# Native float32 products, DVE remainders and other beats in a transform and two-layer MLP kernel

## The chip, the cores and the metric

The kernel runs on one core of a Trainium2 chip. The metric is the device time of one execution in microseconds (us), as the median of a few runs. A core has TensorE (PE in the profile, its weight loads PEld), VectorE (DVE), ScalarE (ACT), GpSimd (POOL) and SyncE (SP), which here only issues DMAs. The engines run side by side and wait for each other through semaphores.

## What is computed

```python
def _attn_ref(x, filt_r, filt_i):              # x: 2 x 3008 x 256
    X = np.fft.rfft(x, axis=1)
    Y = X * (filt_r + 1j * filt_i)[None, :, :]
    return np.fft.irfft(Y, n=x.shape[1], axis=1).astype(np.float32)

def _moe_ref(x, w_in, w_out):                  # 6016 x 256 -> 2048 -> 256
    h = x @ w_in
    g = np.where(h >= 1, h, np.where(h <= -1, 0.0, (h + 1) ** 2 / 4))
    return (g @ w_out).astype(np.float32)

def _moe2_ref(x, w_in, w_out):                 # 6016 x 256 -> 2048 -> 256
    h = x @ w_in
    g = h * (1.0 / (1.0 + np.exp(-h)))
    return (g @ w_out).astype(np.float32)
# output = moe2(moe(attn(x, filt), moe_w_in, moe_w_out), moe2_w_in, moe2_w_out)
```

The convolution over 3008 positions is done as a transform of 47 x 64 points by matrix products; then come two layers of up and down products with an activation between them.

## The kernel before

**Precision.** A product that has to keep float32's accuracy is made in one of two ways. Native: one TensorE product of float32 operands. Split: each operand is written as a rounded part (type float32r, made by ACT) and a remainder (operand minus rounded part), and three fast products are summed: high x high, high x low, low x high. `triple` does this for the layers; `product` chooses between the two for the transform.

**Stages.** The transform works on 32 items (`items`, 16 channel chunks of 2 batches). The first batch (items 0 to 15) is transformed at the head, with native products. The second batch (items 16 to 31) is spread through the first layer as side work: per item one product `fwd_n1` (512 columns), a transpose `turn_fwd`, a product `fwd_n2` (384 columns), the filter `filter_` and `swap_add`, a product `inv_n2` (384 columns) and a transpose `turn_inv` into Z. All side products share one PSUM bank (`bank`, `side[0]`). Before the change the three side products are split ones: `split_x`, `split_st` and `split_item` make the parts in tiles named `hl`, the rounded part on ACT and the remainder on POOL; `split_mats` does it once for the matrices.

**Layers.** Token blocks 0 and 1 of layer 1 go through `up`, `act_rest`, `split_g` and `down`, one weight slice per beat (beats NB to GA), while `read_weight`, `form_weight` and `split_weight` convert layer 1's weights from 64-bit input. Then 88 steps of seven Strassen products each (`step`, `Group`): 40 of layer 1 and 48 of layer 2. A step is four beats. `rest_x2`, `sum_x` and `split_x2` prepare the tokens of the next pair. Layer 2's weights are converted in beats from L2C on (`fetch_weight` to `put_weight`), and from them `stage2`, `sums2`, `round2`, `rest2` and `store2` make the Strassen sums and their parts.

**Order.** What runs when is decided in two layers. The agenda (`at`, `due`) puts each piece of work at a beat. The `Planner` then holds some of the program back: PE's instructions stay in the order of the program, but for each of the others it picks the operation with the earliest modelled start, and one with an earlier due time if it starts little later. `Planner.cost` has the modelled durations. Every instruction is issued from line 179 (`put`), so the profile's rows are told apart by tile names. A modelled flag `port` keeps DVE operations of two SBUF operands and POOL operations apart.

Of the kernel before, what the change touches and what calls it, by code (L numbers as in the profile page):

```python
# [9 lines left out]
F32 = mybir.dt.float32  # L10
# [27 lines left out]
PMAX = 502  # L38
# [66 lines left out]
class Planner:  # L105
# [48 lines left out]
    def cost(self, engine, method, out, ins):  # L154
        n = out[3]
        psum = sum(i[4] for i in ins)
        port = False
        if method == "dma_start":
            return 0.06, 2.2 + 128 * n * 4 / 250e3, False
        if engine == "PE":  # L160
            busy = n / 2400 + 0.019 if "32r" in ins[0][5] else n / 600 + (0.067 if n < 128 else 0)
            return busy, busy + 0.19, False
        if engine == "ACT":
            busy = n / 1400 + (0.11 if psum else 0.152)
            return busy, busy + 0.15, False
        if engine == "DVE":
            busy = n / 960 + 0.065
            if method == "transpose":
                busy = 0.61
            return busy, busy + 0.14, len(ins) - psum >= (1 if method == "tensor_scalar" else 2)  # L170
        busy = n / 425 + 0.06
        return busy, busy + 0.17, True
# [133 lines left out]
def tile_fft_conv_moe_moe(  # L306
# [122 lines left out]
    def split_weight(m, f, pool):  # L429
        a = cv.pop((m, f))  # L430
        wh = pool.tile([128, 512], F32R, tag="wh", name=f"wh{m}_{f}")
        wl = pool.tile([128, 512], F32R, tag="wl", name=f"wl{m}_{f}")
        weights[m, f] = wh, wl
        nc.scalar.activation(wh, a, AF.Copy)
        (nc.vector if f in (0, 1) else nc.gpsimd).tensor_tensor(wl, a, wh.bitcast(F32), ALU.subtract)
# [30 lines left out]
    mats = {}  # L466

    def split_mats():
        for key, a in (("fwd1", fwd1), ("fwd2", fwd2), ("inv2", inv2)):
            hi, lo = (  # L470
                dp.tile([a.shape[0], 128], F32R, name=f"{key}_{s}", bufs=1) for s in ("hi", "lo")
            )
            nc.scalar.activation(hi, a, AF.Copy)
            nc.gpsimd.tensor_tensor(lo, a, hi.bitcast(F32), ALU.subtract)
            mats[key] = hi, lo

    def split_item(i, src):
        p, w = src.shape[0], src.shape[1:]
        hl = rot("raw")
        parts = [hl[:p, j, :w[0] * (w[1] if len(w) > 1 else 1)] for j in range(2)]  # L480
        if len(w) > 1:
            parts = [v.rearrange("p (d k) -> p d k", k=w[1]) for v in parts]
        nc.scalar.activation(parts[0], src, AF.Copy)
        nc.gpsimd.tensor_tensor(parts[1], src, parts[0].bitcast(F32), ALU.subtract)
        return parts

    def split_x(i):
        xt[i] = split_item(i, xt[i])

    def split_st(i):  # L490
        s = st[i]
        st[i] = split_item(i, s[:, :, :K1] if s.shape[2] > K1 else s)

    def product(out, key, matrix, src):
        if not isinstance(src, list):
            nc.tensor.matmul(out, matrix, src, start=True, stop=True)
            return
        (mh, ml), (h, l) = mats[key], src
        nc.tensor.matmul(out, mh, h, start=True, stop=False)
        nc.tensor.matmul(out, mh, l, start=False, stop=False)  # L500
        nc.tensor.matmul(out, ml, h, start=False, stop=True)

    def fwd_n1(i):
        st[i] = bank()
        product(st[i], "fwd1", fwd1, xt.pop(i))
# [10 lines left out]
    def fwd_n2(i):  # L516
        ps = bank()[:, :XS]
        src = st[i] if isinstance(st[i], list) else st[i][:, :, :K1]
        product(ps.rearrange("p (d k) -> p d k", k=K1), "fwd2", fwd2, src)
        st[i] = ps  # L520
# [27 lines left out]
    def inv_n2(i):  # L548
        zb[i] = zps[i % 2] if i < HEAD else bank().rearrange("p (d k) -> p d k", k=32)
        z = zb[i][:, :, :K1]  # L550
        if i in PRODUCT:
            y, v = st.pop(i)
            nc.tensor.matmul(z, inv2_swap, v.rearrange("p (d k) -> p d k", k=K1), start=True, stop=False)
            nc.tensor.matmul(z, inv2, y, start=False, stop=True)
            return
        product(z, "inv2", inv2, st.pop(i))
# [206 lines left out]
    def rest2(j, i):  # L763
        h, q = (flat2(j, hl, i // 2)[:, i % 2 * 448:(i % 2 + 1) * 448] for hl in (1, 0))
        nc.gpsimd.tensor_tensor(q.bitcast(F32R), q, h, ALU.subtract)
# [119 lines left out]
    late_tiles = []  # L885
# [8 lines left out]
    def first_slots():  # L894
        for tag in "gu":
            for i in range(2):
                spare(rings[tag][(turn.get(tag, 0) + 1 + i) % 2])
        spare(rings["we"][0].bitcast(F32))
        spare(wa3)

    def swap_slots():
        rings["wa"].append(wa3)
        for t in (rings["we"][0], wa3):
            retired.append(t.name)
        free[:] = [t for t in free if t.tensor.name not in retired]
        ring[:] = [r for r in ring if r is not xring2]
        nc.release(rings["xb"][1:])
        v = mp.tile([128, 2 * PMAX], F32, tag="xb1", name="sl_xb", bufs=1)
        late_tiles.append(v.name)
        spare(v, 2)  # L910

    def late_slots():
        c = late.tile([128, PMAX], F32, name="c0")
        late_tiles.append(c.name)
        spare(c)
        sets.append(late.tile([128, 2, 2, 7, 128], F32, name="w2e"))

    def raw_slots():
        retired.clear()
        spare(rings["we"][0].bitcast(F32))  # L920
        spare(rings["raw"][0].bitcast(F32), 2)

    def second_slots():
        retired.extend(late_tiles)
        free[:] = [t for t in free if t.tensor.name not in retired]
        spare(rings["wa"][0])
        rings["obl"] = [*rings["ob"][:2], *rings["wa"][1:]]
# [295 lines left out]
    for i in range(AHEAD_F, HEAD):  # L1223
# [12 lines left out]
    B1, SP = GA, 30  # L1236
    BSTAGES = (
        (-6, (load_x,)), (0, (fwd_n1, turn_fwd, split_st)), (7, (inv_n2, turn_inv)),
        (2, (fwd_n2, filter_, swap_add)), (4, (split_st,)), (1, (signs,)),
        (-1, (load_f,)), (-1, (split_x,)),  # L1240
# [6 lines left out]
    at(B1 - 5, split_mats)  # L1247
    END = B1 + SP * (n - 1 - HEAD) // 10 + 8
    L2C = GA + 62
    SOLO = (END - GA) // 4 + 1 | 1  # L1250

    for n_ in range(2, 6):
        for k in range(2):
            at(NB + 2 + 2 * (2 * (n_ - 2) + k), stage_block, n_, k)
# [5 lines left out]
    for j in range(NP):  # L1260
        t, r = ((GA - 14, 3), (GA - 6, 1))[j] if j < 2 else (GA + 4 * (j - 3), 2)
        at(t, sum_first, j)
        at(t + r, round_first, j)
        at(t + r + 1, rest_first, j)
    for f in range(NFC):
        t = L2C + 3 * f
        at(t, fetch_weight, 1, f)
        at(t + 3, read_weight, 1, f)
        at(t + 3, form_weight, 1, f)
        at(t + 5, put_weight, f)  # L1270
# [14 lines left out]
    xring2 = [rings["xb"][1][:, s] for s in range(2)]  # L1285

    def keep_slot():
        nonlocal wa3
        wa3 = rings["wa"].pop()

    wa3 = None
    at(GA - 5, keep_slot)

    def make_xring():
# [3 lines left out]
        ring[7:7] = [[x[:, s] for s in range(2)] for x in rings["xb"][:1]] + [xring2]  # L1298

    at(GA - 14, make_xring)  # L1300
    first = {"B11": -12, "B21": -11, "T2": -8, "T3": -6, "T1": -5, "B22": -3, "T4": -2}
    sums = {"T1": -10, "T2": -9, "T3": -8, "T4": -7}
    later = {"B11": 12, "B21": 14, "T2": 18, "T3": 28, "T1": 28, "B22": 29, "T4": 30}
    sums_later = {"T1": 16, "T2": 17, "T3": 20, "T4": 24}
    nine = {"B11": 12, "B21": 14, "T2": 26, "T3": 28, "T1": 29, "B22": 29, "T4": 30}
    held = END - GA - 4 * NP
    after = {"B11": held + 4, "B21": held + 5, "T2": 27, "T3": 28, "T1": 29, "B22": 29, "T4": 30}
    sums_after = {"T1": held + 6, "T2": held + 6, "T3": held + 7, "T4": held + 7}
    for p in range(len(PL)):
        t = GA + 4 * NP * (p - 1) if p else GA  # L1310
        s = t + 3 if p else GA - 13
# [7 lines left out]
        for which, d in (after if p == 2 else nine if p in (3, 4, 5) else later if p else first).items():  # L1319
            at(t + d, split_x2, p, which)  # L1320
            at(t + d + 1, rest_x2, p, which)
# [45 lines left out]
    def stages(t):  # L1367
        if t == max(NB, DONE + 1):
# [3 lines left out]
            sp = sctx.enter_context(tc.tile_pool(name="sums", bufs=1))  # L1372
            sums_.extend(sp.tile([128, 2, 384], F32R, name=f"sum{i}") for i in range(3))
# [4 lines left out]
        if t == B1 - 6:  # L1378
            nc.release(rings["raw"])
            make_raw("hl", [128, 2, 512], F32R)  # L1380
# [4 lines left out]
    def end_side():  # L1385
# [3 lines left out]
        nc.release(rings["raw"] + [t for m in mats.values() for t in m])  # L1389
        nc.release([t for tag in DP for t in rings[tag] if hasattr(t, "name")])  # L1390
        make_raw("rawb", [128, 512], I64)
# [5 lines left out]
    at(L2C - 2, swap_slots)  # L1397
    at(L2C + 3 * NFC + 8, raw_slots)
# [41 lines left out]
    for q in range(STEPS):  # L1440
# [11 lines left out]
        if q == Q2 + 1:  # L1452
# [3 lines left out]
            v = mp.tile([128, 2, PMAX], F32R, tag="xb1", name="xb2", bufs=1)  # L1456
            ring.insert(0, [v[:, s] for s in range(2)])
# [58 lines left out]
```

## Time and profile before

| | us |
|---|---|
| median of 3 runs | 1094.67 |
| lowest, highest | 1093.49, 1095.71 |
| the profiled execution | 1092.82 |
| its span in the trace | 1091.0 |
| PE busy | 1068.4 |
| DVE busy | 978.3 |
| ACT busy | 926.7 |
| POOL busy | 246.3 |

The busy time of PE is a union of matmul records that overlap: a record of 502 columns shows some 390 ns, while the next one starts about 227 ns later. A stall of PE shows as idle only where it is longer than that overlap, so the time from start to start says more than the busy share. A native float32 product stands as two records. Times in the rows are from the span's start; the layers' first beat lies near 48 us, GA near 148 us, and the side work runs from there to about 328 us.

### The profile page before, as it was taken

The page shows a single profiled execution, that of the slowest core. Times are in us where ns is not written, and L with a number is a line of the kernel's source. Part 1 is how long each engine was busy: PE and PEld are TensorE (multiplying, and loading weights), DVE is VectorE, ACT ScalarE, POOL GpSimd, SP SyncE. Part 2 cuts the span into 40 slices and gives each one's busy share as a digit, 9 for nine tenths or more (in the row PEclk, how much of TensorE's full clock was granted, in tenths as well). Part 3 has the DMA queues.
Part 4 walks back from the last instruction along what each step waited for, and adds up shares of the span by engine and source line. Part 5 has one row for each costly group of instructions (what it writes and reads, how often), then busy time and mean ns, then how long its engine had stood idle before and what let it go on. Part 6 is the DMA issues. An engine that isn't in the chain of part 4 may idle for free.

```text
span 1091.0 us, 14799 instructions
## 1 busy us (share of the span) xinstructions
PE 1068.4 (98%) x4743; PEld 869.1 (80%) x4743; DVE 978.3 (90%) x1579; ACT 926.7 (85%) x1746; POOL 246.3 (23%) x210
## 2 busy tenths in 40 slices
PE   9899989999999999999999999999999999999998
PEld 4588866777778888887888888888888888888886
DVE  7878988998777898999886779999999999999998
ACT  3588878989987989998997889889889889889885
POOL 6544636675540123324230000000000000000000
PEclk9999999999999999999999999999999999999999
DMA  9423232233311456565687452343433334332301
GB/s 352 142 78 126 96 124 92 85 98 114 127 47 46 161 176 212 177 206 182 239 283 266 145 170 83 136 140 112 148 122 116 125 107 140 130 111 102 120 20 39
DMA packets 66702, 149.76 MB, mean 137 GB/s; under 512 B 6848, under 2 KB 31552, under 8 KB 66624
## 3 DMA queue, kind: packets, MB, share of 16 engines
q1 hardware_dynamic: 66192, 148.54, 39.8%
q8 instruction: 37, 0.61, 0.2%
q14 instruction: 41, 0.34, 0.1%
q10 hardware_dynamic: 432, 0.27, 0.1%
HBM read 113.42 MB, written 35.37 MB: 136 GB/s over the span
## 4 chain that ended last, share of the span: by engine, by line
PE 77%; DVE 10%; ACT 9%; issue 2%; DMA 1%; POOL 0%; SPq 0%; DVEq 0%; ACTq 0%; POOLq 0%
PE h L179 39%; PE o_a L179 21%; PE o_b L179 17%; DVE gl L179 2%; ACT gh L179 2%; ACT u L179 1%; DVE wa L179 1%; ACT g L179 1%; DMA Z<-in_x_dram 1%; DVE u L179 1%; ACT wa L179 1%; DVE h L179 1%; DVE g L179 1%; ACT sl_xb L179 1%; ACT we L179 1%
## 5 line engine op out<-in xcount | busy, mean ns | idle before, releaser
L179 PE MATMUL h<-xr,ur 128*128 128x502 f32 (+1 forms) x792 | 220.8, 389 | 0.0
L179 PEld LDWEIGHTS h<-xr,ur 128*128 128x128 f32 x792 | 149.0, 189 | 31.2 <-ACT sl_g L179 0.4
L179 PE MATMUL o_a<-gl,wh 128*128 128x502 f32 (+1 forms) x358 | 139.6, 390 | 1.3 <-DVE gl L179 1.3
L179 PE MATMUL o_a<-gh,wh 128*128 128x502 f32 (+1 forms) x358 | 139.9, 391 | 0.0
L179 PE MATMUL o_a<-gh,wl 128*128 128x502 f32 (+1 forms) x358 | 139.6, 390 | 0.0
L179 PE MATMUL o_b<-gl,wh 128*128 128x502 f32 (+1 forms) x316 | 123.5, 391 | 1.1 <-DVE gl L179 1.0
L179 PE MATMUL o_b<-gh,wh 128*128 128x502 f32 (+1 forms) x316 | 123.6, 391 | 0.0
L179 PE MATMUL o_b<-gh,wl 128*128 128x502 f32 (+1 forms) x316 | 123.2, 390 | 0.0
L179 DVE TENSOR_TENSOR gl<-sl_g,gh 128x502 fp32r<-128x502 f32 (+1 forms) x137 | 90.9, 673 | 5.9 <-ACT gh L179 5.7
L179 ACT ACTIVATE gh<-sl_g 128x502 fp32r<-128x502 f32 (+1 forms) x137 | 83.9, 618 | 10.8 <-PE o_a L179 5.8
L179 PE MATMUL h<-xr,wh 128*128 128x502 f32 (+1 forms) x288 | 89.7, 393 | 1.0 <-ACT h L179 0.5
L179 PE MATMUL h<-xr,sum 128*128 128x502 f32 (+1 forms) x312 | 88.3, 391 | 0.9 <-ACT wa L179 0.5
L179 PEld LDWEIGHTS o_a<-gl,wh 128*128 128x128 f32 x358 | 67.4, 188 | 14.9 <-DVE gl L179 1.9
L179 PEld LDWEIGHTS o_a<-gh,wl 128*128 128x128 f32 x358 | 67.3, 188 | 13.7
L179 PEld LDWEIGHTS o_a<-gh,wh 128*128 128x128 f32 x358 | 67.5, 188 | 13.1
L179 PEld LDWEIGHTS o_b<-gl,wh 128*128 128x128 f32 x316 | 59.5, 188 | 14.0 <-DVE gl L179 2.7
L179 PEld LDWEIGHTS h<-xr,sum 128*128 128x128 f32 x312 | 58.5, 188 | 14.5 <-ACT wa L179 1.8
L179 PEld LDWEIGHTS o_b<-gh,wl 128*128 128x128 f32 x316 | 59.5, 188 | 12.2
L179 PEld LDWEIGHTS o_b<-gh,wh 128*128 128x128 f32 x316 | 59.5, 188 | 11.5
L179 PEld LDWEIGHTS h<-xr,wh 128*128 128x128 f32 x288 | 53.2, 188 | 14.8 <-ACT h L179 1.2
L179 ACT ACTIVATE u<-h 128x502 f32<-128x502 f32 (+1 forms) x94 | 54.8, 582 | 10.6 <-PE h L179 8.2
L179 ACT ACTIVATE u<-u 128x502 f32<-128x502 f32 (+1 forms) x100 | 61.9, 619 | 1.8 <-DVE u L179 0.6
(411 smaller groups left out, 2701.7 us busy)
## 6 DMA issues: line engine op xcount, KB each, us to landing
ur<-w2u SPq DMA_DIRECT2D x48, 896.0 KB, 4.6
f<-in_filt_dram SPq DMA_DIRECT2D x32, 384.0 KB, 3.8
sum<-w1s SPq DMA_DIRECT2D x32, 384.0 KB, 3.1
w2u<-w2s SPq DMA_DIRECT2D x10, 448.0 KB, 4.1
Z<-in_x_dram SPq DMA_DIRECT2D x16, 256.0 KB, 5.6
raw<-in_moe_w_in_dram SPq DMA_DIRECT2D x16, 256.0 KB, 2.7
raw<-in_moe_w_out_dram SPq DMA_DIRECT2D x16, 256.0 KB, 2.9
xin<-in_x_dram SPq DMA_DIRECT2D x16, 256.0 KB, 3.1
```

The lines of the kernel that those rows point to most:

```text
L179: op = Op(engine, lambda: call(*args, **kwargs), busy, until, port)
```

## The change

- The side products become native: `split_x`, `split_st`, `split_item`, `split_mats` and `product` go, with the `hl` tiles. `inv_n2` of an item comes 4 beats after its `fwd_n1` instead of 7 (`INV`), and the side work ends 3 beats earlier (`END`).
- Two kinds of remainder go from POOL to DVE: `split_weight` for slices 2 to 15 of layer 1, and `rest2` for layer 2.
- Layer 2's weights are converted from GA + 50 instead of GA + 62 (`L2C`), one slice every 3.5 beats instead of 3.
- The planner's durations are set anew: POOL, the DVE transpose and DVE's tensor_scalar.
- The stage blocks 2 to 5 are made one per beat instead of one every two; the first pair's sums and parts (`first`, `sums`) and the first weight sums are spread over some 22 beats before GA instead of 12; `make_xring` moves from GA - 14 to GA - 23. The list `nine` goes.
- SBUF slots: one `raw` tile and a new tile `c0` are slots from the start; `keep_slot`, `swap_slots` and `raw_slots` go, and both `xb` tiles stay in the ring of token parts.

```diff
@@ cost
             if method == "transpose":
-                busy = 0.61
+                busy = 0.62
+            elif method == "tensor_scalar":
+                busy = n / 1920 + 0.07
             return busy, busy + 0.14, len(ins) - psum >= (1 if method == "tensor_scalar" else 2)
-        busy = n / 425 + 0.06
+        busy = n / 430 + 0.1
@@ split_weight
-        (nc.vector if f in (0, 1) else nc.gpsimd).tensor_tensor(wl, a, wh.bitcast(F32), ALU.subtract)
+        nc.vector.tensor_tensor(wl, a, wh.bitcast(F32), ALU.subtract)
@@ the transform's products
-        nc.scalar.activation(parts[0], src, AF.Copy)
-        nc.gpsimd.tensor_tensor(parts[1], src, parts[0].bitcast(F32), ALU.subtract)
...
-        nc.tensor.matmul(out, mh, h, start=True, stop=False)
-        nc.tensor.matmul(out, mh, l, start=False, stop=False)
-        nc.tensor.matmul(out, ml, h, start=False, stop=True)
...
-        product(st[i], "fwd1", fwd1, xt.pop(i))
+        nc.tensor.matmul(st[i], fwd1, xt.pop(i), start=True, stop=True)
...
-        product(ps.rearrange("p (d k) -> p d k", k=K1), "fwd2", fwd2, src)
+        nc.tensor.matmul(ps.rearrange("p (d k) -> p d k", k=K1), fwd2, st[i][:, :, :K1], start=True, stop=True)
...
-        product(z, "inv2", inv2, st.pop(i))
+        nc.tensor.matmul(z, inv2, st.pop(i), start=True, stop=True)
@@ rest2
-        nc.gpsimd.tensor_tensor(q.bitcast(F32R), q, h, ALU.subtract)
+        nc.vector.tensor_tensor(q.bitcast(F32R), q, h, ALU.subtract)
@@ the agenda
-    B1, SP = GA, 30
+    B1, SP, INV = GA, 30, 4
     BSTAGES = (
-        (-6, (load_x,)), (0, (fwd_n1, turn_fwd, split_st)), (7, (inv_n2, turn_inv)),
-        (2, (fwd_n2, filter_, swap_add)), (4, (split_st,)), (1, (signs,)),
-        (-1, (load_f,)), (-1, (split_x,)),
+        (-6, (load_x,)), (0, (fwd_n1, turn_fwd)), (INV, (inv_n2, turn_inv)),
+        (2, (fwd_n2, filter_, swap_add)), (1, (signs,)), (-1, (load_f,)),
     )
-    END = B1 + SP * (n - 1 - HEAD) // 10 + 8
-    L2C = GA + 62
-    SOLO = (END - GA) // 4 + 1 | 1
+    END = B1 + SP * (n - 1 - HEAD) // 10 + INV + 1
+    L2C = GA + 50
+    SOLO = (END - GA) // 4 + 2 | 1
-            at(NB + 2 + 2 * (2 * (n_ - 2) + k), stage_block, n_, k)
+            at(NB + 1 + 2 * (n_ - 2) + k, stage_block, n_, k)
-        t, r = ((GA - 14, 3), (GA - 6, 1))[j] if j < 2 else (GA + 4 * (j - 3), 2)
+        t, r = ((GA - 18, 3), (GA - 8, 3))[j] if j < 2 else (GA + 4 * (j - 3), 2)
-        t = L2C + 3 * f
+        t = L2C + 7 * f // 2
-    at(GA - 14, make_xring)
-    first = {"B11": -12, "B21": -11, "T2": -8, "T3": -6, "T1": -5, "B22": -3, "T4": -2}
-    sums = {"T1": -10, "T2": -9, "T3": -8, "T4": -7}
+    at(GA - 23, make_xring)
+    first = {"B11": -22, "B21": -20, "T2": -16, "T3": -13, "T1": -10, "B22": -7, "T4": -4}
+    sums = {"T1": -20, "T2": -19, "T3": -18, "T4": -17}
```

## Rows read from the trace of the kernel before

**Rows 1.** The page: busy time in us, share of the span and instructions by engine.
```profile
PE 1068.4 (98%) x4743; PEld 869.1 (80%) x4743; DVE 978.3 (90%) x1579; ACT 926.7 (85%) x1746; POOL 246.3 (23%) x210
```

**Rows 2.** Windows: length; PE, PEld, DVE, ACT, POOL busy (count); clock; DMA; GB/s.
```profile
48.60:61.00 12.40, 9.87 (x43) 8.01 (x42) 9.84 (x16) 8.92 (x16) 3.88 (x3) 0.86 0.39 129
61.00:136.00 75.00, 75.00 (x372) 63.80 (x371) 65.44 (x101) 62.89 (x120) 40.55 (x31) 1.00 0.30 102
136.00:148.00 12.00, 9.79 (x42) 7.23 (x41) 11.57 (x22) 10.76 (x23) 6.35 (x6) 1.00 0.47 166
148.00:316.00 168.00, 158.15 (x687) 125.61 (x687) 145.61 (x229) 145.84 (x275) 97.90 (x85) 1.00 0.30 97
316.00:580.00 264.00, 263.07 (x1224) 219.51 (x1223) 232.97 (x372) 241.59 (x463) 67.69 (x51) 1.00 0.55 186
600.00:1040.00 440.00, 440.00 (x1938) 364.56 (x1937) 413.10 (x686) 383.64 (x718) 0.00 (x0) 1.00 0.36 125
```

**Rows 3.** PE's largest wait in 148:316: for whom, total us, times, longest.
```profile
PE h L179 <- DVE y L179: 3.2, 3, 1.5
```

**Rows 4.** Timeline of PE, split side products: start, length, instruction, count.
```profile
152.08 0.40 PE L179 MATMUL h<-hl,fwd_lo 128*128 128x512 f32 x1
152.31 0.39 PE L179 MATMUL o_a<-gh,wh 128*128 128x502 f32 x1
...
161.17 0.51 PE L179 MATMUL h<-hl,fwd_hi 128*128 128x384 f32 x2
161.52 0.33 PE L179 MATMUL h<-hl,fwd_lo 128*128 128x384 f32 x1
```

**Rows 5.** Timeline of PE at the head, native products of the first batch.
```profile
29.45 1.02 PE L179 MATMUL h<-Z,fwd 128*128 128x512 f32 x2
30.30 0.81 PE L179 MATMUL h<-t,dft_sb 128*128 128x384 f32 x2
30.95 0.81 PE L179 MATMUL o_b<-y,dft_sb 128*128 128x384 f32 x2
31.59 1.02 PE L179 MATMUL h<-Z,fwd 128*128 128x512 f32 x2
```

**Rows 6.** Window, instructions on tile hl alone: length, PE, PEld, ACT, POOL busy.
```profile
148.00:316.00 168.00, 35.83 (x138) 24.73 (x138) 24.24 (x44) 54.11 (x44) 1.00 0.30 97
```

**Rows 7.** Timeline of POOL, then of DVE, in 442:445.
```profile
442.55 1.16 POOL L179 TENSOR_TENSOR w2e<-w2e 128x448 fp32r<-128x448 f32 x1
...
442.78 1.47 DVE L179 TENSOR_TENSOR gl<-g,gh 128x502 fp32r<-128x502 f32 x1
...
444.75 0.67 DVE L179 TENSOR_TENSOR gl<-h,gh 128x502 fp32r<-128x502 f32 x1
```

**Rows 8.** Groups of POOL that move: busy, mean ns, idle before and its releaser.
```profile
L179 POOL TENSOR_TENSOR w2s<-w2s 128x448 fp32r<-128x448 f32 x20 | 26.1, 1331 | 41.8 <-DMA w2s<-w2d 14.8 <-ACT h L179 7.9 <-ACT g L179 6.8
L179 POOL TENSOR_TENSOR wl<-wa,wh 128x512 fp32r<-128x512 f32 x14 | 19.1, 1366 | 26.8 <-ACT wh L179 26.8
```

**Rows 9.** Timeline of DVE before the layers' first products, and PE's wait there.
```profile
43.17 0.75 DVE L179 TENSOR_SCALAR wa<-wa 128x512 f32<-128x512 f32 x2
44.92 0.72 DVE L179 STREAM_TRANSPOSE Z<-o_b 128x512 f32<-128x512 f32 x1 [1.00 <-PE o_b L179]
45.56 0.65 DVE L179 SCALAR_TENSOR_TENSOR wa<-wa,we 128x512 int32<-128x512 int32 x1
...
50.85 1.70 DVE L179 TENSOR_TENSOR wl<-wa,wh 128x512 fp32r<-128x512 f32 x2
...
PE h L179 <- DVE wl L179: 2.5, 1, 2.5
```

**Rows 10.** Timelines of DVE, ACT and POOL: one item between its two last products.
```profile
181.63 1.01 DVE L179 TENSOR_TENSOR y<-h,f 128x384 f32<-128x384 f32 x2
...
189.33 0.53 ACT L179 ACTIVATE s<-y 64x384 f32<-64x384 f32 x1
...
190.07 1.45 POOL L179 TENSOR_TENSOR s<-y,s 128x384 f32<-128x384 f32 x1
```

More of the change, by code (lines that the diff above doesn't have):

```diff
@@ L464, in load_f @@
         nc.sync.dma_start(ft[i], filt[c])
[L466 to L482, printed above, removed]
-        nc.scalar.activation(parts[0], src, AF.Copy)
-        nc.gpsimd.tensor_tensor(parts[1], src, parts[0].bitcast(F32), ALU.subtract)
[L485 to L498, printed above, removed]
-        nc.tensor.matmul(out, mh, h, start=True, stop=False)
-        nc.tensor.matmul(out, mh, l, start=False, stop=False)
-        nc.tensor.matmul(out, ml, h, start=False, stop=True)
     def fwd_n1(i):
         st[i] = bank()
-        product(st[i], "fwd1", fwd1, xt.pop(i))
+        nc.tensor.matmul(st[i], fwd1, xt.pop(i), start=True, stop=True)
     def turn_fwd(i):
@@ L517, in fwd_n2 @@
         ps = bank()[:, :XS]
-        src = st[i] if isinstance(st[i], list) else st[i][:, :, :K1]
-        product(ps.rearrange("p (d k) -> p d k", k=K1), "fwd2", fwd2, src)
+        nc.tensor.matmul(ps.rearrange("p (d k) -> p d k", k=K1), fwd2, st[i][:, :, :K1], start=True, stop=True)
         st[i] = ps
@@ L884, in tile_fft_conv_moe_moe @@
     Q2 = NP * L2P
-    late_tiles = []
+    c0 = []
     free, retired, groups, parts, banks, touched = [], [], {}, {}, {}, {}
@@ L897, in first_slots, with late_slots, free_slot @@
                 spare(rings[tag][(turn.get(tag, 0) + 1 + i) % 2])
-        spare(rings["we"][0].bitcast(F32))
[L899 to L921, printed above, removed]
+        spare(rings["raw"].pop(0).bitcast(F32), 2)
+        spare(c0[0])
+    def late_slots():
+        sets.append(late.tile([128, 2, 2, 7, 128], F32, name="w2e"))
+    def free_slot():
+        spare(rings["we"][0].bitcast(F32))
     def second_slots():
-        retired.extend(late_tiles)
+        retired.append(c0[0].name)
         free[:] = [t for t in free if t.tensor.name not in retired]
@@ L1246, in tile_fft_conv_moe_moe @@
                 at(t + d, fn, i)
-    at(B1 - 5, split_mats)
-    END = B1 + SP * (n - 1 - HEAD) // 10 + 8
-    L2C = GA + 62
-    SOLO = (END - GA) // 4 + 1 | 1
+    END = B1 + SP * (n - 1 - HEAD) // 10 + INV + 1
+    L2C = GA + 50
+    SOLO = (END - GA) // 4 + 2 | 1
     for n_ in range(2, 6):
         for k in range(2):
-            at(NB + 2 + 2 * (2 * (n_ - 2) + k), stage_block, n_, k)
+            at(NB + 1 + 2 * (n_ - 2) + k, stage_block, n_, k)
     pools = {}
@@ L1283, in tile_fft_conv_moe_moe @@
         at(Y - 24 + 4 * (t // 2), load_down, t)
[L1285 to L1292, printed above, removed]
     def make_xring():
@@ L1297, in make_xring @@
         ring.extend([xr[:, i, s] for s in range(2)] for i in range(8))
-        ring[7:7] = [[x[:, s] for s in range(2)] for x in rings["xb"][:1]] + [xring2]
-    at(GA - 14, make_xring)
-    first = {"B11": -12, "B21": -11, "T2": -8, "T3": -6, "T1": -5, "B22": -3, "T4": -2}
-    sums = {"T1": -10, "T2": -9, "T3": -8, "T4": -7}
+        ring[7:7] = [[x[:, s] for s in range(2)] for x in rings["xb"]]
+    at(GA - 23, make_xring)
+    first = {"B11": -22, "B21": -20, "T2": -16, "T3": -13, "T1": -10, "B22": -7, "T4": -4}
+    sums = {"T1": -20, "T2": -19, "T3": -18, "T4": -17}
     later = {"B11": 12, "B21": 14, "T2": 18, "T3": 28, "T1": 28, "B22": 29, "T4": 30}
     sums_later = {"T1": 16, "T2": 17, "T3": 20, "T4": 24}
-    nine = {"B11": 12, "B21": 14, "T2": 26, "T3": 28, "T1": 29, "B22": 29, "T4": 30}
     held = END - GA - 4 * NP
-    after = {"B11": held + 4, "B21": held + 5, "T2": 27, "T3": 28, "T1": 29, "B22": 29, "T4": 30}
+    after = {"B11": held + 4, "B21": held + 5, "T2": 27, "T3": 28, "T1": 28, "B22": 29, "T4": 30}
     sums_after = {"T1": held + 6, "T2": held + 6, "T3": held + 7, "T4": held + 7}
@@ L1310, in tile_fft_conv_moe_moe @@
         t = GA + 4 * NP * (p - 1) if p else GA
-        s = t + 3 if p else GA - 13
+        s = t + 3 if p else GA - 24
         at(s, load_pair, p)
@@ L1318, in tile_fft_conv_moe_moe @@
             at(t + d, sum_x, p, which)
-        for which, d in (after if p == 2 else nine if p in (3, 4, 5) else later if p else first).items():
+        for which, d in (after if p == 2 else later if p else first).items():
             at(t + d, split_x2, p, which)
@@ L1372, in stages @@
             sp = sctx.enter_context(tc.tile_pool(name="sums", bufs=1))
+            c0.append(sp.tile([128, PMAX], F32, name="c0"))
             sums_.extend(sp.tile([128, 2, 384], F32R, name=f"sum{i}") for i in range(3))
@@ L1377, in stages @@
             fixed["ws"] = rawp.tile([128, 384], F32, tag="ws", name="ws", bufs=1)
-        if t == B1 - 6:
-            nc.release(rings["raw"])
-            make_raw("hl", [128, 2, 512], F32R)
     def begin_side():
@@ L1388, in end_side @@
         rings["obs"] = rings["ob"]
-        nc.release(rings["raw"] + [t for m in mats.values() for t in m])
         nc.release([t for tag in DP for t in rings[tag] if hasattr(t, "name")])
-        make_raw("rawb", [128, 512], I64)
         dctx.close()
@@ L1396, in tile_fft_conv_moe_moe @@
     at(END, end_side)
-    at(L2C - 2, swap_slots)
-    at(L2C + 3 * NFC + 8, raw_slots)
+    at(L2C + 3 * NFC + 8, free_slot)
     for q in range(NP, NP * L2P):
@@ L1455, in tile_fft_conv_moe_moe @@
             sctx.close()
-            v = mp.tile([128, 2, PMAX], F32R, tag="xb1", name="xb2", bufs=1)
-            ring.insert(0, [v[:, s] for s in range(2)])
             gp = ctx.enter_context(tc.tile_pool(name="gp", bufs=1))
```

## The prediction, made before the changed kernel was run

> **What bounds the kernel.** I read the page first. PE is busy for 98% of the span and DVE for 90% [rows 1], so PE sets the time and DVE is close behind. An average hides the stages, so I read the windows next. In 600:1040 PE starts 1938 matmuls in 440 us, 0.227 us each, with no idle time [rows 2]: layer 2 runs at PE's pace and the change hardly touches it. I use that pace as a ruler. The loss of a stage is its length minus what its matmuls would take at full pace.
>
> In 148:316, the side transform, 687 matmuls stand in 168 us [rows 2]. 138 of them are side products [rows 6]. Their pace is on the timeline: a pass of 512 columns takes 0.23 us to the next start, and two passes of 384 take 0.35 us [rows 4]. The 138 are 48 of 512 columns and 90 of 384: 48 x 0.23 + 90 x 0.175 = 26.8 us. The other 549 take 549 x 0.227 = 124.6 us. Together that is 151.4, so **16.6 us are lost** in this stage; only 9.9 of them show as idle. The largest item among PE's waits there is DVE's `y`, the filter of the side work, 3.2 us [rows 3]. ACT and DVE are both busy for 146 of the 168 us [rows 2]: the losses are queues in front of two full engines.
>
> Three smaller places: 136:148 has 42 matmuls in 12 us, 9.5 at full pace, a loss of 2.5 us. In 48.6:61 PE waited 2.5 us for DVE's `wl` [rows 9], and the granted clock averages 0.86 over 12.4 us [rows 2]. Against the levels 2.4 and 1.2 GHz that is 28% of the window, 3.5 us, at the lower one, which costs half of that, 1.7 us. In 316:580 only 0.9 us are idle [rows 2].
>
> **The change part by part.** *Native products.* At the head the same shapes run native: 30.30 - 29.45 = 0.85 us for 512 columns, then 0.65 and 0.64 for 384 [rows 5], 2.14 per item. Split, an item costs 3 x 0.23 + 6 x 0.175 = 1.74. So PE gets 0.40 us more on each of 16 items: **+6.5 us**, all on the path, since PE is the bound. This term is sure.
>
> *The parts of the side work go.* In 148:316 the `hl` tiles hold ACT for 24.2 us and POOL for 54.1 us [rows 6]. Without them ACT is busy for 122 of 168 us (72%, it was 87%) and POOL for 44 instead of 98. DVE's own work stays, yet it gains too: a `gl` remainder on DVE took 1.47 us while POOL ran 442.55 to 443.71, and 0.67 just after [rows 7]. DVE waited for POOL's instruction to end. With over half of POOL's time gone, over half of such waits go. Each item also loses three steps of two engines between its products. What does that give back of the 16.6 us? At most nearly all (16). At the least those losses that have nothing to do with the parts; I put that end at 4. DVE still stands near 85%, and the side products still share one bank whose release waits for DVE, so some losses stay. I take two thirds, **-11 us**, nearer to the upper end, because ACT drops well below full and DVE's waits for POOL shrink at the same time.
>
> *The inverse product comes 3 beats earlier.* It waits for filter, swap and sum. In the trace this chain ran from 181.63 to 191.52 us, 9.9 us, while its own steps are 1.01 + 2 x 0.53 + 1.45 = 3.5 us [rows 10]; the rest is queueing that cost nothing with five beats between the two products. An item of three beats takes some 168 / 16 = 10.5 us, so the two beats that remain are 7 us. The planner picks by due time, so the chain should move up. I cost it at nothing; the cover is 3.5 us of slack, and if it goes, PE stands behind `inv_n2`, since its order is fixed. That is a rival below.
>
> *Remainders from POOL to DVE.* 14 of layer 1 and 32 of layer 2 (20 stand in the row, 12 more on another tile) took POOL 1.37 and 1.33 us each [rows 8]. On DVE one costs at most the 0.67 us of a `gl` [rows 7]: 14 x 0.67 = 9.4 us and 32 x 0.67 x 448/502 = 19 us. In return DVE no longer waits for them. Most of the first lie in 61:136, where DVE is busy for 65.4 of 75 us including such waits [rows 2]; most of the second in 316:580, with 233 of 264. Both still fit. I cost it at 0, with bounds of -1 and +4 for layer 2's part.
>
> *Before GA.* Stage blocks come earlier, the first pair's parts are spread over more beats. The loss of 2.5 us in 136:148 comes with DVE busy for 11.6 of 12 us [rows 2]. Spreading should ease it, but the 9.4 us of remainders arrive just ahead. I cost it at 0, between -2.5 and +3.
>
> *The first weight.* PE's 2.5 us at 48.6 wait for `wl` of slice 0, whose chain passes the row at 45.56, which stands on DVE behind a transpose that had to wait 1.00 us for PE [rows 9]. The planner models a tensor_scalar of 512 elements at 512/960 + 0.065 = 0.60 us; two of them took 0.75 [rows 9]. With the new 0.34 it sees DVE free some 0.8 us earlier and may put that row ahead of the transpose. If it does, wait and slow clock go, -4.2 us at most; if the order stays, 0. I take half, **-2.1**.
>
> *The rest at nothing.* The conversion's DMAs (two loads and a store per slice, on SP's queue) start 12 beats earlier. They move ahead of stores and loads of the same queue where no transfer shows among PE's longer waits, and layer 2's start is 30 us away. One slot more early and two fewer late matter only if a group waits for a slot, and none shows. If a slot or a load does bind, it falls into the +4 above.
>
> **The sum**: 6.5 - 11 - 2.1 = -6.6 us. The profiled execution took 1092.82 us and would come to 1086.2. It lies 1.85 us below the median of the runs, so I add that back: 1094.67 - 6.6 = **1088.1 us**. All low ends: 6.5 - 16 - 1 - 2.5 - 4.2 = -17.2, 1077. All high ends: 6.5 - 4 + 4 + 3 + 0 = +9.5, 1104.
>
> **Rivals.** *The inverse product becomes the wait.* If the chain keeps 7.9 us or so, PE stands 0.9 us for each of 16 items, +14 on the forecast: 1102. For it speaks the 9.9 us now; against it, that due times shorten it and that ACT and POOL have room. It decides from a chain of 7 us on.
>
> *PE pays and nothing comes back.* The side work stalls for DVE and the shared bank as before, and the change does not do what lighter ACT and POOL promise: 1094.7 + 6.5 = 1101. For it speaks that the longest wait is one for DVE [rows 3], whose own work stays; against it, DVE's waits for POOL.
>
> *Half comes back.* 8 us instead of 13 meet the 6.5: 1093.
>
> *DVE becomes the bound.* In 61:136 there are 9.6 us of room [rows 2]; 9.4 us of remainders and several 0.67 us parts of the first pair come in. From the point where DVE's work exceeds the stage, the surplus goes to PE: some 5 us at the most, 1093, and with as much again in 316:580, 1098. Against it speak the waits for POOL that vanish. The Trainium skill, Perfetto Trace Analysis, section Optimizing Scalar/DVE Operations, says that with a saturated DVE work may be offloaded, even to GpSimd; by that the change moves work the wrong way. The same section adds that the two share a read port, so that moving between them might not help. The trace agrees with that addition (1.47 against 0.67 us [rows 7]), so this rival gets a small chance.
>
> **How the numbers follow.** Forecast, 1079 to 1092: 0.61. Below that, when the losses go almost wholly: 0.05. Half comes back: 0.10. DVE bound: 0.08, split between no change and slower. Inverse product: 0.09. Nothing back: 0.07. Some 0.2%, 2.2 us, is about what a measurement of this kernel can tell from no change. Faster by more: 0.61 + 0.05 = 0.66. Within: 0.10 + 0.04 = 0.14. Slower: 0.04 + 0.09 + 0.07 = 0.20. The range leaves out 0.05 below and most of the last two cases above: 1079 to 1100.
>
> **What would show it.** In the changed profile the side products stand at 0.86 and 0.65 us to the next start. The side stage should lose under 8 us beside them, with ACT below 80%. PE's wait for `y` should shrink; waits of `h` for `s` or `ob`, POOL's sums, would show the first rival. Waits for `wl` in 61:136 would show DVE as the bound. At 48 us the wait for `wl` is gone or stays. 600:1040 should keep 0.227 us per matmul; if that moved, the prediction would be wrong in a place that I did not look at.

## The result and the profile after

| | before | after |
|---|---|---|
| median of 4 runs, us | 1094.13 | 1076.91 |
| lowest, highest | 1093.49, 1095.71 | 1076.50, 1077.55 |
| span of the profiled execution | 1091.0 | 1075.8 |

The ratio is 0.9841, with a 95% interval of 0.9824 to 0.9858: 17.2 us less, where 6.6 had been forecast. The sign was right; the time lies below the range of 1079 to 1100. The two profiled executions, which the rows come from, differ by 15.3 us (1092.82 and 1077.55). Some 1 to 2 us of the 17.2 (an estimate) are TensorE at its lower clock in other executions of the kernel before: 31 of 55 that were run beside the experiments had a mean granted clock of 0.998 or more and a median of 1093.1 us, 19 had 0.996 or less and 1094.9, and the changed kernel's eight all had 0.999 or 1.00.

The page of the changed kernel, its line of busy times, against [rows 1]. POOL's time has halved; PE has 48 instructions less (144 records of split side products became 96 of native ones) and the same busy time.

```profile
PE 1067.3 (99%) x4695; PEld 862.9 (80%) x4695; DVE 962.1 (89%) x1625; ACT 901.3 (84%) x1695; POOL 122.7 (11%) x113
```

Windows of the changed kernel, for [rows 2] (columns as there; the stages begin up to 6 us earlier). In the side stage, the fourth row, PE is busy for 166.5 of 168 us instead of 158.2; ACT, POOL and DVE all have less to do. Ahead of it, the first row has full clock and no idle time, and in the second PE shows no idle time either, with DVE busy for 65.6 of 68 us.

```profile
49.20:61.60 12.40, 12.40 (x74) 11.03 (x73) 10.28 (x19) 11.61 (x21) 3.46 (x3) 1.00 0.27 91
61.60:129.60 68.00, 68.00 (x330) 57.49 (x329) 65.56 (x119) 60.54 (x116) 20.63 (x17) 1.00 0.33 107
129.60:141.60 12.00, 11.60 (x52) 9.28 (x50) 11.95 (x25) 8.63 (x18) 2.91 (x4) 1.00 0.51 185
141.60:309.60 168.00, 166.54 (x671) 125.71 (x672) 136.94 (x228) 130.38 (x243) 41.95 (x40) 1.00 0.32 104
600.00:1040.00 440.00, 439.99 (x1938) 364.46 (x1938) 417.53 (x694) 385.50 (x722) 0.00 (x0) 1.00 0.35 121
```

PE's waits in that side stage, for [rows 3]: the wait for `y` went from 3.2 us to 0.4.

```profile
PE h L181 <- DVE gl L181: 1.2, 2, 0.7
PE h L181 <- DVE y L181: 0.4, 1, 0.4
```

A native product in the changed kernel's timeline of PE, for [rows 5]. It is read differently from the head: the next matmul starts in the records 0.46 us after the product and then lasts 0.80 instead of 0.39, so part of the product hides in it. To the second next start it is 167.75 - 166.66 = 1.09 us; less one pace of 0.227 that is 0.86 for 512 columns, as priced.

```profile
166.66 1.02 PE L181 MATMUL h<-xin,fwd 128*128 128x512 f32 x2
167.12 0.80 PE L181 MATMUL o_b<-gh,wh 128*128 128x500 f32 x1
167.75 0.39 PE L181 MATMUL o_b<-gl,wh 128*128 128x500 f32 x1
```

DVE before the layers' first products, timeline, for [rows 9]. The row that formed the first weight (SCALAR_TENSOR_TENSOR, at 45.56 before) now stands ahead of the transpose, at 44.43, and `wl` follows at 47.98 instead of 50.85. PE no longer waits for it.

```profile
44.43 0.68 DVE L181 SCALAR_TENSOR_TENSOR wa<-wa,we 128x512 int32<-128x512 int32 x1
45.52 0.72 DVE L181 STREAM_TRANSPOSE Z<-o_b 128x512 f32<-128x512 f32 x1 [0.41 <-PE o_b L181]
...
47.98 0.69 DVE L181 TENSOR_TENSOR wl<-wa,wh 128x512 fp32r<-128x512 f32 x1
```

**Where the time went, stage by stage.** For this table I took every matmul's time to the next start, subtracted its shape's pace (0.226 us for 502 columns, 0.43 and 0.323 for one of the two records of a native product of 512 and 384, the others likewise), and summed what is left by stage. GA is the start of the first Strassen step. "All but native" and the columns behind it are experiments that follow below. The side stage runs from GA to its last side product.

| lost us in | before | after | all but native | native alone | durations alone | remainders alone | beats alone |
|---|---|---|---|---|---|---|---|
| head | 4.4 | 5.0 | 4.3 | 5.1 | 5.1 | 4.4 | 4.6 |
| first 13 us of the layers | 4.6 | 0.5 | 0.5 | 5.7 | 0.4 | 4.6 | 1.9 |
| from there to GA - 12 us | 1.2 | 0.9 | 0.9 | 1.2 | 1.7 | 1.4 | 9.5 |
| last 12 us before GA | 3.0 | 0.7 | 0.0 | 1.8 | 1.0 | 2.3 | 1.3 |
| side stage | 18.3 | 4.2 | 19.6 | 5.8 | 23.2 | 22.6 | 19.9 |
| side stage to layer 2 | 5.3 | 3.6 | 4.0 | 5.4 | 7.4 | 3.3 | 5.4 |
| layer 2 | 3.8 | 3.8 | 3.8 | 3.8 | 3.7 | 3.8 | 3.8 |

Before to after: 40.6 - 18.7 = 21.9 us less lost, 6.5 more for native products: 15.4, and the spans differ by 15.2.

A loss counted in this way holds the time that TensorE spends at its lower clock level, 1.2 GHz. In the side stage the granted clock was 1.00 before and after. "All but native", the durations alone and the remainders alone had 0.98, 0.99 and 0.97 there: 6.8, 3.4 and 10.2 us at the lower level, of which half is lost, 3.4, 1.7 and 5.1 us. With the remainders alone the clock fell behind waits of PE for DVE's `gl` of 2.1 us (it stood at 0.54 in 148.5:156) and 2.7 us.

### The profile page after: what moved, and what is told of

It is laid out like the page before. It is cut to its first block, busy times and chain, and to the rows that moved or that the text cites. A ratio compares the mean times of both kernels' runs of the same rounds, so it can differ in the third digit from the quotient of the medians.

```text
span 1075.8 us, 14491 instructions
## 1 busy us (share of the span) xinstructions
PE 1067.3 (99%) x4695; PEld 862.9 (80%) x4695; DVE 962.1 (89%) x1625; ACT 901.3 (84%) x1695; POOL 122.7 (11%) x113
## 4 chain that ended last, share of the span: by engine, by line
PE 93%; DVE 3%; ACT 2%; DMA 1%; issue 0%; POOL 0%; SPq 0%; DVEq 0%; ACTq 0%; POOLq 0%
PE h L181 48%; PE o_a L181 24%; PE o_b L181 21%; ACT u L181 1%; DVE gl L181 1%; DMA f<-in_filt_dram 1%; DVE wa L181 1%; DVE h L181 1%; ACT gh L181 0%; DVE xr L181 0%; DMA fwd<-in_dft_dram 0%; DVE ws L181 0%; ACT raw L181 0%; DVE Z L181 0%; DVE y L181 0%
## 5 line engine op out<-in xcount | busy, mean ns | idle before, releaser
L181 PE MATMUL h<-xr,ur 128*128 128x502 f32 (+1 forms) x816 | 227.9, 389 | 0.0
L181 PEld LDWEIGHTS h<-xr,ur 128*128 128x128 f32 x816 | 153.4, 188 | 32.3 <-ACT sl_g L181 0.4
L181 PE MATMUL o_a<-gh,wh 128*128 128x502 f32 (+1 forms) x358 | 147.8, 413 | 0.0
L181 PE MATMUL o_b<-gh,wh 128*128 128x502 f32 (+1 forms) x316 | 130.8, 414 | 0.0
L181 PE MATMUL h<-xr,sum 128*128 128x502 f32 (+1 forms) x336 | 94.5, 390 | 0.1
L181 PEld LDWEIGHTS o_a<-gh,wh 128*128 128x128 f32 x358 | 67.5, 189 | 16.6 <-issue 1.4
L181 PEld LDWEIGHTS o_a<-gh,wl 128*128 128x128 f32 x358 | 67.4, 188 | 14.1
L181 PE MATMUL h<-xr,wh 128*128 128x502 f32 (+1 forms) x240 | 74.4, 391 | 0.1
L181 PEld LDWEIGHTS h<-xr,sum 128*128 128x128 f32 x336 | 63.3, 189 | 13.5 <-ACT u L181 0.5
L181 POOL TENSOR_TENSOR wa<-wa,raw 128x512 int32<-128x512 int32 x32 | 46.1, 1440 | 185.6 <-DVE wa L181 142.0
L181 DVE TENSOR_TENSOR gl<-h,gh 128x502 fp32r<-128x502 f32 (+1 forms) x84 | 56.7, 674 | 9.1 <-ACT gh L181 8.3
```

The source lines that it names most:

```text
L181: op = Op(engine, lambda: call(*args, **kwargs), busy, until, port)
```

## The experiments

Each median is compared with runs of the kernel before on the same chip (1092.9 to 1094.3 us). Four theories went in. S: making the side parts is the cause. P: the planner's old durations are. L: POOL's instructions keep DVE waiting. B: a backlog from before GA is.

### One edit alone on the kernel before

Native products alone: the split steps leave the agenda, `product` finds no parts.

```diff
-        (-6, (load_x,)), (0, (fwd_n1, turn_fwd, split_st)), (7, (inv_n2, turn_inv)),
-        (2, (fwd_n2, filter_, swap_add)), (4, (split_st,)), (1, (signs,)),
-        (-1, (load_f,)), (-1, (split_x,)),
+        (-6, (load_x,)), (0, (fwd_n1, turn_fwd)), (7, (inv_n2, turn_inv)),
+        (2, (fwd_n2, filter_, swap_add)), (1, (signs,)), (-1, (load_f,)),
...
-    at(B1 - 5, split_mats)
```

> The kernel before with native side products alone: the parts (hl tiles) are not made, the inverse product stays 7 beats after the first, nothing else changes. Theory S (the parts were the cause: ACT's and POOL's time on them and the longer chain): PE loses at most 3 us in the side stage instead of 16.6 and pays 6.5 more, so about 1087 us. Theory P (the planner's old durations misplace the side work, with or without parts): the losses stay and PE pays, about 1100 us. Theory L (it is POOL's hold on DVE that costs, and native takes half of POOL's time in the stage away): half of the loss goes, about 1092 us.

Measured 1085.9 us, a ratio of 0.9931 (0.9913 to 0.995) on 1093.4. The trace is that of a second run of the same kernel, which took 1087.4:

> The kernel before with native side products alone, again, for its trace. The time should be near 1086. If the theory of POOL's hold is right, the side stage loses 5 to 7 us instead of 18, the wait for wl at 48 us and its 4 us stand as before, and the loss between the side stage and layer 2 stands at 5.

The side stage loses 5.8 us instead of 18.3, and the other stages nearly what they lost before. The time is just below what S expected (1087). P, which expected 1100, falls, and L's "half of the loss" (1092) was too little. This edit alone brings 7.5 of the 17.2 us: -12.5 in the side stage, +6.5 on PE, and the rest lies within the scatter of the executions (the second run was 1.5 us longer).

The durations alone (the first hunk of the diff), the remainders alone (`split_weight`, `rest2`), the beats alone (stage blocks, `first`, `sums`, the first weight sums, `make_xring`, the first `load_pair`):

> The kernel before with the new modelled durations alone. Theory S: only the order at 48 us changes, the first wl is in time and wait and slow clock go there: -4 us, about 1090. Theory P: the side stage loses less too, -10 us or more, 1084 or below. Theory L: as S.

> The kernel before with the remainders of layer 1's slices and of layer 2's Strassen sums on DVE alone. Theory S: no change in the side stage, within 1.5 us of before. Theory L: DVE gains more from the locks that go than the remainders cost it, -2 to -4 us, in 61:136 and 316:580. If DVE were the bound there: +3 to +6 us.

> The kernel before with the new beats before GA alone (stage blocks one per beat, first sums and parts spread over 22 beats, the ring of parts earlier). Theory S: only the 2.5 us of 136:148 can go, about 1092. A theory B, that the backlog built up before GA runs on into the side stage: -6 us or more, 1088 or below. If DVE and ACT are too full in 85:136 for the earlier parts: +2 us.

Measured 1093.4 (ratio 1.0000, 0.999 to 1.0009), 1095.4 (1.0009, 0.9995 to 1.0024) and 1098.5 (1.005, 1.0035 to 1.0065). The durations do remove the 4.2 us at the first weight and 2.0 in the last 12 us before GA, but the side stage takes 4.9 back (1.7 of it is the clock) and the stretch behind it 2.1. The remainders alone do gain 2.0 us in that stretch, where most of them lie, but lose 4.3 in the side stage, where 5.1 us go to the lower clock. The beats alone lose 8.3 us more in the beats up to GA - 12, and 4.1 more up to GA in all; of the 9.5 us lost there 5.9 are one wait, for a converted weight, and some 3.6 the lower clock behind it (0.95 granted over 78 us). PE's waits of that kernel in 61.8:139.9:

```profile
PE h L179 <- ACT wh L179: 5.9, 1, 5.9
```

So none of these three gains anything alone, where S had expected 4 us of the durations and L 2 to 4 of the remainders. B falls: with the durations alone the layers lose 3.1 us before GA instead of 8.8, and the side stage loses more and not less.

### All but one

> The kernel before with the new durations, both kinds of remainder on DVE and the new beats before GA, but with the split side products. Theory F (the side stage is full as long as the parts are made, and gives back there what is gained ahead of it): head and beats before GA lose some 6 us less than before, the side stage more, and the time stays at 1091 to 1095. A theory A (the edits add up, native only its own share of 8): 1076.9 + 8 = 1085.

Measured 1087.2 (0.9941, 0.9925 to 0.9958), between the two theories. 7.4 us less are lost in the layers before GA, and the side stage loses 19.6, 1.3 more than before (3.4 of it is the clock). So most was kept: "a full side stage gives it all back" was too strong. That the remainders alone lose 4.3 us more there is covered by the clock; of the 4.9 with the durations alone it covers 1.7, and the rest is not explained. PE's longest waits in it are still those for DVE's `gl` and `y`.

The changed kernel with one part undone:

> The changed kernel with the old modelled durations. Theory F: now nothing is given back, so the wait and the slow clock at 48 us return in full, +4, and the order before GA costs +1: about 1082. Theory A: +0 to +1, as the durations alone brought 0.0 to the kernel before: 1077 to 1078.

> The changed kernel with both kinds of remainder back on POOL. Theory L2 (the earlier beats need DVE free of POOL's locks, since the new beats alone lost 8 us more in the beats up to GA - 12 than before): +6 to +10, 1083 to 1087, lost in 62:130. If the remainders on DVE are neutral, as they were alone: 1076 to 1078.

> The changed kernel with the old beats before GA. If spreading the first pair's work is what empties the stretch before GA: the loss of 2 to 3 us in the last 12 us before GA returns, 1079 to 1080. If the native side work and the remainders do that by themselves: within 1 us of 1077.

Measured 1079.4, 1080.3 and 1077.2 us, against 1076.9 (1076.7 on a third chip, below). Old durations cost 2.5, between the two theories; their interval (0.985 to 0.9879) just overlaps that of the changed kernel. DVE takes the rows of the first weight in the old order again, behind the transpose, and the wait for the first `wl` returns, but as 1.2 us instead of 2.5, and with no fall of the clock. The remainders on POOL cost 3.4 (0.9875, 0.986 to 0.9889), about half of the least that L2 expected, 1.6 of it up to GA - 12. The beats cost or bring nothing once the rest is there, though alone they had cost 5.

### What in the side parts costs

The base is the kernel before with new durations, remainders on DVE, new beats before GA and native products (`c_native`), everything but the inverse product's place, layer 2's beats, the slots and the list `nine`.

> The kernel before with the new durations, remainders on DVE, the new beats before GA and native side products, the parts not made; the inverse product stays 7 beats after the first, layer 2's weights and the slots stay as before. If native is what empties the side stage, with or without the earlier inverse product: 1076 to 1079, the side stage loses 4 to 6 us. If the inverse product's place and layer 2's beats have a share: 1080 or more.

Measured 1078.1, as the first theory expected. What it lacks is worth 1.2 us at most as measured; the ratio's interval (0.9836 to 0.9866) overlaps that of the changed kernel, so it is not shown to be worth anything. Then the side parts are made again, but nobody reads them (the products stay native):

```diff
-        xt[i] = split_item(i, xt[i])
+        split_item(i, xt[i])
...
-        st[i] = split_item(i, s[:, :, :K1] if s.shape[2] > K1 else s)
+        split_item(i, s[:, :, :K1] if s.shape[2] > K1 else s)
```

> As c_native, but the side parts are still made, on ACT and POOL, and nobody reads them. Theory W (the time that the parts take on ACT and POOL, with POOL's hold on DVE, is the cause): the side stage loses 12 us or more again, 1085 or above. Theory K (the longer chain from one side product to the next is the cause): as c_native, within 2 us.

Measured 1091.9, +13.9 us, for work that nothing waits for. The longer chain is not the cause, since the products no longer pass through the parts; making them is. Then each engine by itself:

```diff
 c_act_only
-        nc.gpsimd.tensor_tensor(parts[1], src, parts[0].bitcast(F32), ALU.subtract)
 c_pool_only
-        nc.scalar.activation(parts[0], src, AF.Copy)
-        nc.gpsimd.tensor_tensor(parts[1], src, parts[0].bitcast(F32), ALU.subtract)
+        nc.gpsimd.tensor_tensor(parts[1], src, src, ALU.subtract)
```

> As c_native, with ACT's rounded parts made and unused, POOL's remainders not made. If ACT's fullness is the cause: close to c_parts_unused. If POOL's hold on DVE is: close to c_native, +1 to +2 us.

> As c_native, with a subtraction on POOL for each side part (source minus itself, unused), ACT's rounded parts not made. If POOL's hold on DVE is the cause: +6 us or more over c_native. If ACT's fullness is: +1 to +2 us.

Measured 1079.4 (+1.3) and 1088.0 (+9.9). One window, 148:300, of `c_native`, then `c_act_only`, then `c_pool_only`, columns as in [rows 2]. ACT takes 137.5 of 152 us in the second, 90%, and PE hardly notices. In the third ACT has least to do, and PE loses 5 us of busy time. DVE's instructions get longer there: 129.29 us for 197 of them, 0.656 on average, against 124.76 for 208, 0.600. Of the 9.9 us 1.7 are the lower clock (3.4 us of it, behind the wait of 2.2 us for `y` below). The two prices do not add up to 13.9. One reason may be that a source minus itself is shorter than the real remainder: 1.02 us each on POOL in this window, against 1.26 in `c_parts_unused`.

```profile
148.00:300.00 152.00, 150.21 (x608) 113.86 (x607) 124.76 (x208) 120.28 (x220) 41.75 (x39) 1.00 0.34 105
```

```profile
148.00:300.00 152.00, 149.96 (x604) 112.98 (x604) 122.69 (x207) 137.53 (x264) 41.01 (x39) 1.00 0.33 105
```

```profile
148.00:300.00 152.00, 145.13 (x571) 107.02 (x570) 129.29 (x197) 114.14 (x208) 84.90 (x80) 0.99 0.33 103
```

PE's longest waits in the same window, of `c_native`, then of `c_pool_only`: the longest are for DVE.

```profile
PE h L181 <- DVE t L181: 1.3, 1, 1.3
PE h L181 <- DVE y L181: 0.4, 1, 0.4
```

```profile
PE h L181 <- DVE y L181: 2.9, 3, 2.2
PE h L181 <- DVE t L181: 1.8, 2, 1.4
```

Does POOL keep DVE waiting, or is its own queue too long for the side chain? The same places on POOL and the same tiles, modelled with the same duration and the same `port` flag, but written only:

```diff
-        nc.gpsimd.tensor_tensor(parts[1], src, src, ALU.subtract)
+        n = parts[0].shape[1] * (w[1] if len(w) > 1 else 1)
+        nc.gpsimd.memset(hl[:p, :, :n].bitcast(F32), 0.0)
```

> As c_pool_only, but each of the 48 POOL subtractions is a memset of both halves of the same unused tile, modelled with the same duration: POOL's queue is as long in the plan, nothing is read. If POOL's reads hold DVE: back near c_native, within 3 us of 1078. If POOL's longer queue delays the side chain: near c_pool_only, 1085 or above.

Measured 1079.9, +1.8 instead of +9.9. Its window, columns as above:

```profile
148.00:300.00 152.00, 149.19 (x598) 111.40 (x597) 123.34 (x206) 118.54 (x217) 69.27 (x77) 1.00 0.33 104
```

The memsets are shorter (0.81 us on average; the subtractions took 0.83 to 1.04 undisturbed and 1.02 on average), so POOL's queue is shorter too, and the time alone does not rule it out. But DVE's instructions are back at 0.599 us on average, as they were without any work of POOL on the side parts. How much of the 8 us the shorter queue gave is open. Two timelines show single ones. `c_pool_only`, POOL then DVE, twice: beside a subtraction a `gl` of two SBUF operands takes 1.46 us; another, whose `h` lies in PSUM, takes 0.64.

```profile
198.18 1.03 POOL L181 TENSOR_TENSOR hl<-xin 128x512 fp32r<-128x512 f32 x1
198.29 1.46 DVE L181 TENSOR_TENSOR gl<-wa,gh 128x500 fp32r<-128x500 f32 x1
...
265.74 0.83 POOL L181 TENSOR_TENSOR hl<-s 128x384 fp32r<-128x384 f32 x1
265.81 0.64 DVE L181 TENSOR_TENSOR gl<-h,gh 128x502 fp32r<-128x502 f32 x1
```

`c_pool_memset`, POOL then DVE: beside a memset a `gl` of two SBUF operands takes 0.67, as if alone. The whole traces agree: the 17 `gl` of two SBUF operands that start while POOL runs a subtraction or another reading instruction in `c_pool_only` took 0.70 us at least and 1.19 in the median, the 10 with an operand in PSUM at most 0.68, and the 7 beside a memset in `c_pool_memset` at most 0.67.

```profile
259.61 1.42 POOL L183 MEMSET hl<- 128x768 f32 x2
...
260.35 0.67 DVE L183 TENSOR_TENSOR gl<-u,gh 128x500 fp32r<-128x500 f32 x1
```

The Trainium skill, SBUF — State Buffer, section Who interferes with whom, says just this: a DVE instruction with two SBUF inputs contends with a GpSimd instruction that reads SBUF, and not with one that only writes. These rows agree in both halves.

### Does DVE have room for the parts?

The split products kept, their remainders on DVE, the other edits as in `b_all_but_native`:

```diff
-        nc.gpsimd.tensor_tensor(parts[1], src, parts[0].bitcast(F32), ALU.subtract)
+        nc.vector.tensor_tensor(parts[1], src, parts[0].bitcast(F32), ALU.subtract)
```

> The kernel before with new durations, new beats before GA and all remainders on DVE, those of the side parts too; the side products stay split, so PE keeps its 6.5 us. If POOL's hold was all and DVE has room for some 25 us more in the side stage: 1071 to 1074. If DVE becomes full, at 83% before it: the side stage loses 8 us or more, 1076 to 1086.

Measured 1091.7, worse than with the remainders on POOL (1087.2) and above both theories. The side stage loses 25.3 us. Its window 148:300:

```profile
148.00:300.00 152.00, 141.23 (x594) 108.69 (x593) 136.61 (x231) 126.22 (x238) 39.57 (x36) 0.99 0.29 97
```

So the parts can't be had for nothing on either engine, and PE's 6.5 us for native products are the cheapest of the three ways tried. That DVE is full at 137 of 152 us, 90%, is not shown: in 600:1040 of the changed kernel it is busy for 95%, and PE does not idle. PE's longest waits here are all for DVE (`wa` and `gl` 2.0 us each, `hl` 1.8, `y` 1.7); whether DVE lacks the time or takes its work in the wrong order was not tested.

### Is anything left?

The changed kernel with the sign products of the side items on DVE, then the swap's sums too, and the changed kernel again:

```diff
-        nc.gpsimd.tensor_tensor(v, v, sgn.unsqueeze(1).to_broadcast([128, DC, K1]), ALU.mult)
+        engine = nc.gpsimd if i < HEAD else nc.vector
+        engine.tensor_tensor(v, v, sgn.unsqueeze(1).to_broadcast([128, DC, K1]), ALU.mult)
...
-            nc.gpsimd.tensor_tensor(s, yf, s, ALU.add)
+            nc.vector.tensor_tensor(s, yf, s, ALU.add)
```

> The changed kernel with the sign products of the side items on DVE instead of POOL (16 of some 1.1 us on POOL, 0.5 us on DVE). If POOL's hold on DVE is still what costs in the side stage: -1 to -3 us, 1074 to 1076. If the rest is DVE's own work: 0 to +1.

> The changed kernel with the sign products and the swap sums of the side items on DVE (32 instructions of some 1.1 us on POOL, 0.5 us on DVE). If POOL's hold is all that is left: the side stage loses 2 to 3 us instead of 4.2, 1074 to 1076. If DVE is full with them (15 us more in a stage where it was busy for 126 of 152): as the changed kernel or above, 1077 to 1080.

> The changed kernel once more, unaltered, for a comparison on one chip: 1077, within 1 us.

Measured 1076.0 (0.9833, 0.9818 to 0.9847), then 1077.1 (0.9857, 0.9843 to 0.9872) and 1076.7 (0.9856, 0.9839 to 0.9872). The last two shared a chip and are equal. In 148:300 POOL was busy for 7.7 us instead of 40.7 and DVE for 131.4 instead of 125.5, and the time is the same; that DVE's own work now costs what POOL's hold did would fit, but what is left was not separated further. The first was measured on another chip; its interval overlaps that of the changed kernel, so no version is shown to beat it.

## Why the prediction was wrong in size

By the table of losses the change brings 15.4 us, where 6.6 were forecast. The 8.8 us between the two lie in four terms: the parts 3.1, the first weight 2.0, the last beats before GA 2.3, the rest of layer 1 1.7 (the head and the beats up to GA - 12 make up the difference). What lies between 15.4 and the 17.2 of the medians is told with the result.

**Native products, +6.5.** Right: 0.86 us for 512 columns, and the account by stages closes with it.

**The parts go, -11.** This step was mis-sized; the stage gave back 14.1 (18.3 to 4.2). Up to 1.7 of the 3.1 us is that I counted the loss in 148:316, 16.6 us, while the stage ran on to about 328. The rest is the share: I took two thirds on the ground that DVE stays near 85% and some losses with it, and I named ACT's relief first. The runs turn that round: ACT's rounded parts alone cost 1.3 us, POOL's subtractions alone 9.9, both together 13.9. At 125 of 152 us DVE still lets PE run, and in 600:1040 at 418 of 440. What had to go was POOL's hold, which the prediction had in its rows as 1.47 against 0.67 us [rows 7], and which it did not price: more than half of POOL's 98 us in the stage [rows 2] went.

**The first weight, -2.1.** The mechanism came exactly as described, rows in the order that was named, and the whole 4.1 us went, wait and slow clock. I took half only because I could not tell the planner's choice. The durations are not the only edit that helps there: with the old ones the changed kernel waits 1.2 us and not 2.5.

**Remainders to DVE, 0.** Wrong in the company of the rest: undoing them costs 3.4 us. Alone they bring nothing in sum, but not for the reason that I had worked out: 2.0 us are gained behind the side stage, and in the side stage 5.1 go to a lower clock. The term hangs on the other edits, and I priced it without them.

**Before GA, 0, and the rest of layer 1, 0.** Measured -2.3 and -1.7. I credited the beats with a possible gain before GA, but with the old beats the changed kernel loses as little there (some 0.5 us); with the durations alone or the native products alone it is already less than before. The 1.7 behind the side stage go with the remainders: alone they gain 2.0 there, where my bounds were -1 and +4.

**The inverse product three beats earlier, 0.** Right as far as can be seen (layer 2's beats and the slots were undone with it, and all of it costs at most 1.2 us): the changed kernel has no wait for the swap's sum among PE's waits. The rival that put 14 us there did not come. Nor did DVE become the bound in 61:136: in 61.6:129.6 PE shows no idle time in the changed kernel, although DVE is at 66 of 68 us.

**The range.** The measured -17.2 us is the sum of all my low ends. That the two agree to the tenth is chance: the side stage gave back 14.1 and not 16, the rest of layer 1 gave more than 1, and some 1 to 2 us are not in the traces' account at all. But most low ends did come true together. I had treated them as separate chances. In the side stage, at the first weight and just before GA PE's longest waits were all for DVE, so one cause may have served all of them; no run separates that. The range should have reached to 1077.

## What to carry to other kernels

Price work on POOL by what it keeps DVE from doing: 48 subtractions of about 1 us that nobody read cost the whole kernel 9.9 us. Where several open terms wait for the same engine, their low ends may come together: give that a case of its own, not a tail that needs luck four times. An edit measured alone can be worth nothing, or less, and still be worth several microseconds beside another that frees the same engine: measure it by undoing it too. And look at the granted clock of each stage before explaining a loss: behind the wait of 2.1 us with the remainders alone, 6.8 us at the lower level cost another 3.4.

## What the runs showed of the hardware

- DVE with two SBUF operands waits for a POOL instruction that reads (1.46 us for a `gl` in `c_pool_only`) and not for one that only writes (0.67 in `c_pool_memset`); with one operand in PSUM it doesn't wait either (0.64 in `c_pool_only`).
- A matmul behind a native float32 product shows a start that is too early and a length that is too long (0.80 instead of 0.39 us); only the sum over two starts tells what the product took.
- A wait of PE of 2.5 us at the layers' start was followed by the clock's lower level, 1.2 GHz (0.86 granted over 12.4 us [rows 2]); one of 1.2 us at the same place, with the old durations in the changed kernel, was not (1.00 over the execution). Length alone does not settle it: in "all but native" the clock fell at 181.6 us behind a wait of 2.7 us, and again at 208.9, where PE's waits were 0.7 and 1.4 us.
